# Chunk-selecting attention and a mixture of experts: rows of tokens placed into expert tables during the attention instead of gathered after it

## The chip, the cores and the metric

The kernel runs on one core of a Trainium2 chip. The metric is the device time of one execution in microseconds. Before the change it is 395.49 us (median of 3 runs, 395.29 to 395.6). A core has five engines that run side by side and meet at semaphores: TensorE (PE) multiplies matrices into PSUM; VectorE (DVE) and ScalarE (ACT) work on tiles in SBUF and PSUM; GpSimd (POOL) works on SBUF and issues DMAs, among them indirect ones, whose rows are picked by a list of indices; SyncE (SP) issues plain DMAs. Sixteen DMA engines move the data.

## The reference, cut to what matters

Attention: 4 batches, 8 heads, 768 positions, 64 channels. Keys lie in 24 chunks of 32. For each query an upper bound of its score against each chunk is computed from the chunk's smallest and largest keys, the 6 chunks with the largest bounds are kept, and a causal softmax attention runs over those alone.

```python
ub = np.sum(np.maximum(q[:, :, :, None, :] * k_min[:, :, None, :, :], q[:, :, :, None, :] * k_max[:, :, None, :, :]), axis=-1)
ub = np.where(causal, ub, -1000000000.0)
top_chunks = np.argsort(ub, axis=-1)[..., -top_k:]
scores = scale * np.matmul(q, k.transpose(0, 1, 3, 2))
mask = sel & (pos[:, None] >= pos[None, :])
# ... softmax over the masked scores, times v
```

Its outputs are 3072 tokens of 512 channels. Each goes through a dense two-layer network and through one of 8 expert networks of the same shape, the one with the largest logit:

```python
y_dense = np.maximum(x @ w1_dense, 0.0) @ w2_dense
expert_idx = np.argmax(x @ w_gate, axis=1)
# for each expert e, over the tokens that chose it (mask):
h = np.maximum(x[mask] @ w1[e], 0.0)
y_moe[mask] = gate_w[mask, None] * (h @ w2[e])
# ...
return y_dense + y_moe
```

The experts' tokens are worked on in blocks of 128 rows of one expert. With any split of 3072 tokens over 8 experts there are at most 24 + 7 = 31 blocks.

## The kernel before

It has three stages. First, attention, two heads ("a pair") at a time, 16 pairs, 11 "units" of scores each. While a batch's attention runs, the dense work of the batch before it is filled in. Then the last batch's dense work and the routing. Then 31 blocks of expert work.

Loading and casting of a pair, and what is prepared from it:

```python
def load(p):
    # ... for k, q, v and both heads:
    nc.sync.dma_start(out=f[:, g], in_=src[b, 2 * hp + g].rearrange("(t p) d -> p t d", p=128))

def cast(p):
    # ... three GpSimd copies from fp32 to fp16: k16, q16, v16

def prep_k(p):
    # ... six transposes of k16 into pk, in PSUM
    nc.vector.tensor_reduce(out=ks[:, 0, :], in_=pkc, op=ALU.max, axis=mybir.AxisListType.X)
    nc.vector.tensor_reduce(out=ks[:, 1, :], in_=pkc, op=ALU.min, axis=mybir.AxisListType.X)
    # ...
    nc.vector.tensor_copy(kT[p % NB][0][64:128, :], pk[0:64])
    nc.vector.tensor_copy(kT[p % NB][1][0:64, :], pk[64:128])

# prep_q: transposes of q, its positive part by ScalarE, its negative part by VectorE
# prep_ub: bounds by matmuls, VectorE's max of 8 for the sixth largest, flags of dropped chunks
# prep_s: twelve transposes (six for each head) and a 128x768 copy for each head
```

Scores, outputs and the end of a pair. The flags lie beside the queries in the moving matrix and rows of -30000 beside the keys, so that dropped chunks vanish in the exponential:

```python
def scores(p, u):
    # ... matmuls of up to 512 columns into sp
    nc.scalar.activation(ex[:, :o], sp[:, :o], AF.Exp, scale=0.125)
    # ... where a tile lies on the diagonal:
    nc.gpsimd.affine_select(out=exd, in_=exd, compare_op=ALU.is_ge, fill=0.0, base=0,
                            pattern=[[0, n], [1, 128]], channel_multiplier=-1)

def av(p, u):
    if u == 0:
        s["op"] = pout.tile([128, 2, 512], FP, name="op")   # pout has one buffer
    # ... matmuls of ex with v into op

def norm(p):
    nc.vector.reciprocal(rs, opv[:, :, :, D : D + 1])
    nc.vector.tensor_tensor(xbig[...], opv[:, :, :, 0:D], rs.to_broadcast([128, 2, NT, D]), ALU.mult)
```

A batch's tokens and dense outputs are stored to two DRAM tensors, `xd` (fp16 rows and the gate's weight) and `yd` (fp32). After attention the routing finds, from one-hot matrices of all 3072 tokens, the list of tokens of every block, and the blocks run:

```python
def gather(i):
    nc.gpsimd.indirect_dma_start(out=xg, in_=xd, in_offset=...gi[:, i : i + 1]...)
    nc.gpsimd.indirect_dma_start(out=yg, in_=yd, in_offset=...gi[:, i : i + 1]...)

# tx(i): four transposes of xg, copied to SBUF by VectorE
# e1(i): four matmuls with the expert's first weights, relu by ScalarE
# th(i): four transposes, copied by ScalarE

def e2(i):
    # ... four matmuls with the expert's second weights into yp
    nc.vector.scalar_tensor_tensor(o, yp, s["x"][:, Dm : Dm + 2].bitcast(FP), s["y"], ALU.mult, ALU.add)
    nc.gpsimd.indirect_dma_start(out=out, out_offset=...si[:, i : i + 1]..., in_=o, ...)

gather(0); gather(1); tx(0)
for i in range(NBLK):
    e1(i)
    # ... gather(i + 2), tx(i + 1), e2(i - 1)
    th(i)
```

The offset of a block's expert in the weights is in a register of PE, all 31 loaded at once before the blocks.

Of the kernel before, what the change touches and what calls it, by code (L numbers as in the profile page):

```python
# [17 lines left out]
def kernel(  # L18
# [31 lines left out]
    xd = dram.tile([N, XW], U16, name="xd")  # L50
    yd = dram.tile([N, Dm], FP, name="yd")
# [4 lines left out]

    exf = const.tile([32, S], HF)
    nc.gpsimd.memset(exf, -30000.0)
    nc.gpsimd.affine_select(out=exf, in_=exf, compare_op=ALU.is_ge, fill=0.0,
                            base=0, pattern=[[1, S]], channel_multiplier=-32)  # L60
    nc.gpsimd.affine_select(out=exf, in_=exf, compare_op=ALU.is_ge, fill=0.0,
                            base=31, pattern=[[-1, S]], channel_multiplier=32)

    cbias = const.tile([128, NT, 2, NC], HF)
    nc.gpsimd.memset(cbias, 0.0)
    for g in range(2):
        nc.gpsimd.affine_select(out=cbias[:, :, g, :], in_=cbias[:, :, g, :], compare_op=ALU.is_ge,
                                fill=-60000.0, base=0, pattern=[[128, NT], [-32, NC]], channel_multiplier=1)


    hmask = const.tile([128, 2, NC], HF)
    nc.gpsimd.memset(hmask, 0.0)
    nc.gpsimd.memset(hmask[0:64, 0, :], 1.0)
    nc.gpsimd.memset(hmask[64:128, 1, :], 1.0)

    NB = 3
    kT = [[const.tile([128, S], HF, name=f"kT{i}_{g}") for g in range(2)] for i in range(NB)]
    q16 = [const.tile([128, NT, 256], HF, name=f"q16_{i}") for i in range(NB)]
    v16 = [const.tile([128, 2, NT, D + 1], HF, name=f"v16_{i}") for i in range(NB)]
    for i in range(NB):  # L80
        nc.vector.memset(kT[i][0], 0.0)
        nc.vector.memset(kT[i][1], 0.0)
        nc.vector.tensor_copy(kT[i][0][0:32, :], exf)
        nc.vector.tensor_copy(kT[i][1][64:96, :], exf)
        nc.gpsimd.memset(q16[i], 0.0)
        nc.gpsimd.memset(v16[i][:, :, :, D : D + 1], 1.0)
# [3 lines left out]
    nc.gpsimd.iota(iom8, pattern=[[0, NT], [1, E]], base=-E, channel_multiplier=0, allow_small_or_imprecise_dtypes=True)  # L90
    ohp = const.tile([128, E, NM + 1], HF)
    nc.gpsimd.memset(ohp, 0.0)
    segm = const.tile([128, E, NM + 1], FP)
    nc.gpsimd.memset(segm, 1.0)
    nc.gpsimd.memset(segm[:, :, 0:1], 0.0)
    ones = const.tile([128, 128], HF)
    nc.gpsimd.memset(ones, 1.0)
    low = const.tile([128, 128], HF)
    nc.gpsimd.memset(low, 1.0)
    nc.gpsimd.affine_select(out=low, in_=low, compare_op=ALU.is_gt, fill=0.0,  # L100
                            base=0, pattern=[[1, 128]], channel_multiplier=-1)
    io128 = const.tile([128, 128], HF)
    nc.gpsimd.iota(io128, pattern=[[1, 128]], base=0, channel_multiplier=0, allow_small_or_imprecise_dtypes=True)
    ioblk = const.tile([128, NBLK], HF)
    nc.gpsimd.iota(ioblk, pattern=[[1, NBLK]], base=0, channel_multiplier=0, allow_small_or_imprecise_dtypes=True)
    iom1 = const.tile([128, NM], HF)
    nc.gpsimd.iota(iom1, pattern=[[1, NM]], base=1, channel_multiplier=0, allow_small_or_imprecise_dtypes=True)
    iop = const.tile([128, 1], FP)
    nc.gpsimd.iota(iop, pattern=[[0, 1]], base=0, channel_multiplier=1, allow_small_or_imprecise_dtypes=True)

    xbig = const.tile([128, NM, XW], HF)
    nc.gpsimd.memset(xbig[:, :, Dm:XW], 0.0)
# [6 lines left out]
    def load_dense():  # L119
        nc.gpsimd.dma_start(out=wg, in_=moe_w_gate.rearrange("(ko ki) e -> ki ko e", ki=128))  # L120
        nc.gpsimd.dma_start(out=wd[:, 0:NK], in_=moe_w1_dense.rearrange("(ko ki) f -> ki ko f", ki=128))
        nc.gpsimd.dma_start(out=wd[:, NK:], in_=moe_w2_dense.rearrange("(ko ki) f -> ki ko f", ki=128))

    def load_expert(e, w):
        src = moe_w1 if w == 0 else moe_w2
        nc.gpsimd.dma_start(out=we[:, e, w * NK : (w + 1) * NK], in_=src[e].rearrange("(ko ki) f -> ki ko f", ki=128))
# [3 lines left out]
    PIECES = [  # L130
        [(0, 0, 512)],
        [(1, 128, 640)],
        [(0, 512, 768), (4, 512, 768)],
        [(2, 256, 768)],
        [(1, 640, 768), (3, 384, 768)],
    ]
    units = []
    for pc in PIECES:
        for g in range(2):
            units.append([(g,) + x for x in pc])  # L140
    units.append([(g, 5, 640, 768) for g in range(2)])
    first_of = {}
    last_of = {}
    for u, un in enumerate(units):
        o = 0
        for g, bb, a, z in un:
            for t in range(a // 128, z // 128):
                last_of[g, t] = (u, bb)
    NU = len(units)

    mh = ctx.enter_context(tc.tile_pool(name="mh", bufs=2))
    my = ctx.enter_context(tc.tile_pool(name="my", bufs=3))
    mg = ctx.enter_context(tc.tile_pool(name="mg", bufs=2))
    mx = ctx.enter_context(tc.tile_pool(name="mx", bufs=2))

    fills = []
# [14 lines left out]

    def batch_fills(b):
# [4 lines left out]
        def xtr(mi):  # L177
            def f():
                tp = ptile("tr", [128, NK, 128], HF, "tp")
                for ko in range(NK):  # L180
                    nc.tensor.transpose(tp[:, ko], xbig[:, b * NT + mi, ko * 128 : (ko + 1) * 128], ident)
                nc.vector.tensor_copy(xT[:, :, mi * 128 : (mi + 1) * 128], tp)
            return f

        def gate():
            lg = ptile("tr", [128, NT, E], FP, "lg")
            for mi in range(NT):
                for ko in range(NK):
# [12 lines left out]
            nc.vector.tensor_tensor(ohp[:, :, 1 + b * NT : 1 + (b + 1) * NT].rearrange("p e t -> p t e"),  # L201
                                    iom8, mn.unsqueeze(2).to_broadcast([128, NT, E]), ALU.is_equal)
            ss = mg.tile([128, NT, 1], FP, name="ss")
            nc.vector.tensor_reduce(out=ss, in_=el, op=ALU.add, axis=mybir.AxisListType.X)
            nc.vector.reciprocal(xbig[:, b * NT : (b + 1) * NT, Dm : Dm + 2].bitcast(FP), ss)
            nc.sync.dma_start(out=xd[b * S : (b + 1) * S].rearrange("(m p) w -> p m w", p=128),
                              in_=xbig[:, b * NT : (b + 1) * NT].bitcast(U16))
# [14 lines left out]
        def l2(g, i, hold):  # L222
            def f():
# [7 lines left out]
                nc.sync.dma_start(out=yd[m * 128 : (m + 1) * 128], in_=ys)  # L231
# [12 lines left out]
        return out_list, dense  # L244

    with (
        tc.tile_pool(name="aload", bufs=3) as aload,
        tc.tile_pool(name="ahead", bufs=2) as ahead,
        tc.tile_pool(name="aexp", bufs=5) as aexp,
        tc.tile_pool(name="psc", bufs=3, space=bass.MemoryType.PSUM) as psc,  # L250
        tc.tile_pool(name="pout", bufs=1, space=bass.MemoryType.PSUM) as pout,
# [3 lines left out]
        st = [dict() for _ in range(NP)]  # L255

        def load(p):
            b, hp = divmod(p, HP)
            for nm, src in (("k", k), ("q", q), ("v", v)):
                f = aload.tile([128, 2, NT, D], FP, name=nm + "f")  # L260
                st[p][nm] = f
                for g in range(2):
                    nc.sync.dma_start(out=f[:, g], in_=src[b, 2 * hp + g].rearrange("(t p) d -> p t d", p=128))

        def cast(p):
# [3 lines left out]
            nc.gpsimd.tensor_copy(q16[p % NB][:, :, 64:192].rearrange("p t (g d) -> p t g d", g=2),  # L269
                                  s["q"].rearrange("p g t d -> p t g d"))  # L270
            nc.gpsimd.tensor_copy(v16[p % NB][:, :, :, 0:D], s["v"])

        def prep_k(p):
            s = st[p]
            pk = pprep.tile([128, S], HF, name="pp")
            for t in range(NT):
                nc.tensor.transpose(pk[:, t * 128 : (t + 1) * 128], s["k16"][:, t].rearrange("p g d -> p (g d)"), ident)
            ks = ahead.tile([128, 2, NC], HF, name="ks")
            pkc = pk.rearrange("d (c w) -> d c w", w=32)
            nc.vector.tensor_reduce(out=ks[:, 0, :], in_=pkc, op=ALU.max, axis=mybir.AxisListType.X)  # L280
            nc.vector.tensor_reduce(out=ks[:, 1, :], in_=pkc, op=ALU.min, axis=mybir.AxisListType.X)
            s["kb"] = kb = ahead.tile([128, 2, 2, NC], HF, name="kb")
            nc.vector.tensor_tensor(kb, ks.unsqueeze(2).to_broadcast([128, 2, 2, NC]),
                                    hmask.unsqueeze(1).to_broadcast([128, 2, 2, NC]), ALU.mult)
            nc.vector.tensor_copy(kT[p % NB][0][64:128, :], pk[0:64])
            nc.vector.tensor_copy(kT[p % NB][1][0:64, :], pk[64:128])

        def prep_q(p):
            s = st[p]
            pq = pprep.tile([128, S], HF, name="pp")  # L290
            for t in range(NT):
                nc.tensor.transpose(pq[:, t * 128 : (t + 1) * 128], q16[p % NB][:, t, 64:192], ident)  # L292
            s["qp"] = qp = ahead.tile([128, S], HF, name="qp")
            nc.scalar.activation(qp, pq, AF.Relu)  # L294
# [131 lines left out]
        while wq:  # L426
            load_expert(*wq.pop(0))
# [180 lines left out]
```

## Time and profile before

| | |
|---|---|
| time | 395.49 us, median of 3 runs |
| span of the profiled execution | 392.8 us |
| busy: PE, DVE, ACT, POOL | 258.8, 192.1, 159.7, 208.0 us |
| moved by DMA | 56.92 MB in 98370 packets, 78462 of them under 512 B |
| attention, first scores to last pair's end | 28.2 to 213.4 us |
| routing and the last batch's dense work | 213.4 to 238.6 us |
| blocks, first transposes to last result | 238.6 to 383.8 us |

The profile is one execution. Its rows of tenths cut the span into 40 slices of 9.8 us: a digit is an engine's busy share there. A group line has a source line, engine, operation, output and input with shapes and a count; then busy time and mean duration; then how long the engine was idle just before these instructions, and who ended that. A timeline line has start and duration in us first, and in brackets the idle time before it and who ended it. Shares over the whole span say little here: the stages have different limits.

### The profile page before, as it was taken

The page shows a single profiled execution, that of the slowest core. Times are in us where ns is not written, and L with a number is a line of the kernel's source. Part 1 is how long each engine was busy: PE and PEld are TensorE (multiplying, and loading weights), DVE is VectorE, ACT ScalarE, POOL GpSimd, SP SyncE. Part 2 cuts the span into 40 slices and gives each one's busy share as a digit, 9 for nine tenths or more (in the row PEclk, how much of TensorE's full clock was granted, in tenths as well). Part 3 has the DMA queues.
Part 4 walks back from the last instruction along what each step waited for, and adds up shares of the span by engine and source line. Part 5 has one row for each costly group of instructions (what it writes and reads, how often), then busy time and mean ns, then how long its engine had stood idle before and what let it go on. Part 6 is the DMA issues. An engine that isn't in the chain of part 4 may idle for free. (4 is left out here: it accounts for less than half of the span.)

```text
span 392.8 us, 7052 instructions
## 1 busy us (share of the span) xinstructions
PE 258.8 (66%) x2426; PEld 152.8 (39%) x2426; DVE 192.1 (49%) x538; ACT 159.7 (41%) x303; POOL 208.0 (53%) x370
## 2 busy tenths in 40 slices
PE   0157377157599989999898872667555658565660
PEld 0135254045365666666665531333222323222230
DVE  8284438248387798777952890222222323232220
ACT  1016257056276867787675320322132222322230
POOL 9946185174455555554322025366756656666541
PEclk9998869779699999999999996888989996989895
DMA  9999999999997886211031425143444444444440
GB/s 182 208 222 214 208 204 198 170 199 204 222 236 191 190 200 145 94 53 56 3 119 49 164 106 173 42 154 114 131 133 132 149 145 135 134 136 133 128 121 0
DMA packets 98370, 56.92 MB, mean 145 GB/s; under 512 B 78462, under 2 KB 90750, under 8 KB 98336
## 3 DMA queue, kind: packets, MB, share of 16 engines
q1 hardware_dynamic: 81856, 28.42, 32.8%
q0 software_dynamic: 16480, 28.06, 30.1%
q8 instruction: 20, 0.33, 0.3%
q14 instruction: 14, 0.11, 0.1%
HBM read 50.08 MB, written 17.66 MB: 172 GB/s over the span
## 5 line engine op out<-in xcount | busy, mean ns | idle before, releaser
L334 ACT ACTIVATE ex<-sp 128x512 f16<-128x512 f32 (+1 forms) x176 | 91.7, 585 | 63.1 <-PE sp L330 31.1
L344 POOL TENSOR_SCALAR_AFFINE_SELECT ex<-ex 128x128 f16<-128x128 f16 (+1 forms) x176 | 52.2, 306 | 55.9 <-ACT ex L334 53.0
L362 PE MATMUL op<-v,ex 128*128 128x65 f16 x672 | 47.6, 200 | 34.6 <-POOL ex L344 29.7
L330 PE MATMUL sp<-r,kT 128*128 128x512 f16 (+3 forms) x256 | 65.1, 328 | 3.6 <-ACT ex L334 2.1
L362 PEld LDWEIGHTS <-ex 128*128 128x128 f16 x672 | 37.3, 101 | 49.5 <-POOL ex L344 35.0
L535 DVE COPY exT<-tp 128x512 f16<-128x512 f16 x31 | 13.2, 425 | 80.5 <-PE tp L533 59.3
L523 POOL DMA_INDIRECT xg<-xd,gi x31 | 30.3, 977 | 41.5 <-DVE yo L561 21.6
L552 ACT COPY ehT<-tp 128x512 f16<-128x512 f16 x31 | 18.2, 586 | 74.2 <-PE tp L550 67.9
L541 PE MATMUL hp<-we,exT 128*128 x124 | 37.4, 432 | 10.2 <-DVE exT L535 5.8
L558 PE MATMUL yp<-we,ehT 128*128 x124 | 38.8, 419 | 4.5 <-ACT ehT L552 2.6
L533 PE MATMUL tp<-ident,xg 128*128 128x128 f16 x124 | 14.2, 247 | 40.7 <-DMA xg<-xd,gi 40.7
L562 POOL DMA_INDIRECT out_dram<-yo,si x31 | 31.5, 1015 | 15.3 <-issue 13.4
L561 DVE SCALAR_TENSOR_TENSOR yo<-yp,xg,yg 128x512 f32<-128x512 f32 x31 | 23.3, 750 | 31.9 <-PE yp L558 27.2
L526 POOL DMA_INDIRECT yg<-yd,gi x31 | 29.4, 949 | 10.5 <-issue 10.2
L322 DVE COPY r<-pp 128x768 f16<-128x768 f16 x32 | 17.0, 554 | 32.8 <-PE pp L320 32.6
L544 ACT ACTIVATE eh<-hp 128x512 f16<-128x512 f32 x31 | 18.5, 597 | 35.2 <-PE hp L541 26.3
L533 PEld LDWEIGHTS <-xg 128*128 128x128 f16 x124 | 8.3, 108 | 56.9 <-DMA xg<-xd,gi 56.8
L217 PE MATMUL hp<-xT,wd 128*128 128x384 f16 x128 | 26.5, 325 | 0.7 <-ACT hT L219 0.3
L330 PEld LDWEIGHTS <-kT 128*128 128x128 f16 x256 | 21.8, 103 | 11.1 <-issue 8.2
L226 PE MATMUL yp<-wd,hT 128*128 128x512 f16 x96 | 24.6, 378 | 1.5 <-DVE xbig L371 1.0
L269 POOL CAST q<-qf 128x768 f16<-128x768 f32 x16 | 13.3, 831 | 21.5 <-DMA qf<-in_q_dram 20.9
L294 ACT ACTIVATE qp<-pp 128x768 f16<-128x768 f16 x16 | 13.0, 810 | 23.1 <-PE pp L292 23.1
(115 smaller groups left out, 431.0 us busy)
## 6 DMA issues: line engine op xcount, KB each, us to landing
we<-in_moe_w_dram POOLq DMA_DIRECT2D x16, 512.0 KB
kf<-in_k_dram SPq DMA_DIRECT2D x32, 192.0 KB, 4.4
qf<-in_q_dram SPq DMA_DIRECT2D x32, 192.0 KB, 4.5
vf<-in_v_dram SPq DMA_DIRECT2D x32, 192.0 KB, 4.7
yd<-ys SPq DMA_DIRECT2D x24, 256.0 KB, 2.1
xd<-xbig SPq DMA_DIRECT2D x4, 792.0 KB, 4.3
wd<-in_moe_w_dense_dram POOLq DMA_DIRECT2D x2, 512.0 KB
xg<-xd,gi POOLq DMA_INDIRECT x31
```

Of the source, the lines that this page charges most:

```text
L217: nc.tensor.matmul(hp, wd[:, ko, j * 128 : (j + 1) * 128], xT[:, ko, g * G * 128 : (g + 1) * G * 128], start=(ko == 0), stop=(ko == NK - 1))
L226: nc.tensor.matmul(yp, hold["h"][:, j, i * 128 : (i + 1) * 128], wd[:, NK + j], start=(j == 0), stop=(j == NK - 1))
L330: nc.tensor.matmul(sp[:, o : o + z - a], kT[p % NB][g][:, bb * 128 : (bb + 1) * 128], s["r", g][:, a:z], start=(o == 0), stop=True, skip_g ...
L334: nc.scalar.activation(ex[:, :o], sp[:, :o], AF.Exp, scale=0.125)
L344: nc.gpsimd.affine_select(out=exd, in_=exd, compare_op=ALU.is_ge, fill=0.0, base=0, pattern=[[0, n], [1, 128]], channel_multiplier=-1)
L362: nc.tensor.matmul(op[:, g, t * (D + 1) : (t + 1) * (D + 1)], ex[:, c : c + 128], v16[p % NB][:, g, bb, :], start=(u == g and n == 0), sto ...
L523: nc.gpsimd.indirect_dma_start(out=xg, out_offset=None, in_=xd, in_offset=bass.IndirectOffsetOnAxis(ap=gi[:, i : i + 1], axis=0))
L526: nc.gpsimd.indirect_dma_start(out=yg, out_offset=None, in_=yd, in_offset=bass.IndirectOffsetOnAxis(ap=gi[:, i : i + 1], axis=0))
L541: nc.tensor.matmul(hp, s["xT"][:, ko], wef[:, bass.ds(offs[i] + ko * 512, 512)], start=(ko == 0), stop=(ko == NK - 1))
L558: nc.tensor.matmul(yp, s["hT"][:, j], wef[:, bass.ds(offs[i] + (NK + j) * 512, 512)], start=(j == 0), stop=(j == NK - 1))
L561: nc.vector.scalar_tensor_tensor(o, yp, s["x"][:, Dm : Dm + 2].bitcast(FP), s["y"], ALU.mult, ALU.add)
L562: nc.gpsimd.indirect_dma_start(out=out, out_offset=bass.IndirectOffsetOnAxis(ap=si[:, i : i + 1], axis=0), in_=o, in_offset=None, bounds_c ...
```

## The change

It rebuilds how tokens reach their experts, and a good part of the attention around it.

1. **A table in place of lists.** DRAM holds one table with room for every token under each expert. When a batch's gate is known, each of its tokens gets its row: its expert's base and its rank among the tokens so far. Six indirect DMAs, one for each tile of 128 tokens, write fp16 rows, gate weight and token number there; each is issued behind a causal mask of the scores, at intervals, during the next batch's attention. The last batch's are issued behind blocks' outputs.
2. **Blocks are plain reads.** 128 rows of the table are read by SyncE at an address in a register, up to eight blocks ahead. The first N1 = 11 blocks are full with tokens of the first three batches and start without the last batch. Blocks 29 to 31 run only where they are needed.
3. **Outputs are added.** The dense outputs are stored straight into the output; a block's result is scaled and added to it by an indirect DMA that accumulates. `yd`, its gathers and the two-operand end of a block go.
4. **The last batch** has its dense work, gate and placing spread over the first blocks.
5. **Attention.** Tokens are laid out so that a partition reads two neighbouring rows of k and q at once (512 B; v stays at 256 B). The transposed keys are copied to SBUF once by ScalarE and reduced there. The flags of both heads share one tile (six transposes for twelve). All four of the first diagonal tiles of a head lie in one unit, so that there are three masks of 512 columns for a pair in place of eleven smaller ones. Outputs lag one unit behind, into a PSUM tile for each head, two in all.
6. **Start.** The first two pairs' loads are issued before the constants; constants of the routing come in pair 2; weights are loaded from pair 1 (dense) and pairs 2 to 13 (experts), each tied to a cast.

The core of the diff, cut:

```diff
-    xd = dram.tile([N, XW], U16, name="xd")
-    yd = dram.tile([N, Dm], FP, name="yd")
+    CAP = N + 128
+    EMPTY = E * CAP
+    table = dram.tile([EMPTY + 128, XW], U16, name="table")
+    N1 = (N * (B - 1) // B - E * 127 + 127) // 128
+    N2 = NBLK - N1
...
+                    nc.sync.dma_start(out=f[:, g].rearrange("p (T j) d -> p T (j d)", j=NJ),
+                                      in_=src[b, 2 * hp + g].rearrange("(T p j) d -> p T (j d)", p=128, j=NJ))
...
+    def expand(i):
+        nc.scalar.copy(kT[i][0][64:96, :], exf[0:32])
+        nc.scalar.copy(kT[i][1][0:32, :], exf[0:32])
...
+        def ranks():
+            # one-hot rows times a triangle of ones, plus bases and counts so far: each token's row
...
+        def place(t):
+            def f():
+                with tc.issue_after(latest["pool"].ins):
+                    put(t)
+            return f
+        def put(t):
+            sc = nc.gpsimd.indirect_dma_start(
+                out=table, out_offset=bass.IndirectOffsetOnAxis(ap=keep["slot"][:, t : t + 1], axis=0),
+                in_=xbig[b % 2][:, t].bitcast(U16), in_offset=None)
...
-                nc.sync.dma_start(out=yd[m * 128 : (m + 1) * 128], in_=ys)
+                for j in range(NJ):
+                    st_ = nc.sync.dma_start(out=outv[m, j], in_=ys[64 * j : 64 * j + 64])
...
+        at.setdefault(9, []).append(ranks)
+        for t in range(NT):
+            at.setdefault(11 + 5 * t, []).append(place(t))
...
+    def fetch(i):
+        es[i]["x"] = xg = eg.tile([128, XW], U16, name="xg")
+        ld = nc.sync.dma_start(out=xg, in_=table[bass.ds(rows[i], 128)])
...
-        tc.tile_pool(name="pout", bufs=1, space=bass.MemoryType.PSUM) as pout,
+        tc.tile_pool(name="pout", bufs=2, space=bass.MemoryType.PSUM) as pout,
...
+            s["kp"] = kp = ahead.tile([128, S], HF, name="kp")
+            nc.scalar.copy(kp.rearrange("d (T p j) -> d T p j", p=128, j=NJ),
+                           pk.rearrange("d (T j p) -> d T p j", p=128, j=NJ))
...
-                nc.gpsimd.affine_select(out=exd, in_=exd, compare_op=ALU.is_ge, fill=0.0, base=0,
-                                        pattern=[[0, n], [1, 128]], channel_multiplier=-1)
+            if pc[0][1] == pc[0][2]:
+                latest["pool"] = nc.gpsimd.affine_select(out=ex, in_=ex, compare_op=ALU.is_ge, fill=0.0, base=0,
+                                        pattern=[[0, 4], [1, 2], [2, 64]], channel_multiplier=-1)
...
-            nc.vector.scalar_tensor_tensor(o, yp, s["x"][:, Dm : Dm + 2].bitcast(FP), s["y"], ALU.mult, ALU.add)
+            nc.vector.tensor_scalar(o, yp, s["x"][:, Dm : Dm + 2].bitcast(FP), None, ALU.mult)
+            sc = nc.gpsimd.indirect_dma_start(
+                out=out, ..., in_=o, ..., compute_op=ALU.add)
...
+        extra = {0: a[:NT] + [a[NT], ranks], 1: places[:2], 2: places[2:4], 3: places[4:] + [empty]}
+        for n, f in enumerate(d):
+            extra.setdefault(1 + n * (N1 - 2) // len(d), []).append(f)
```

## The prediction, made before the changed kernel ran

> **What bounds the kernel now.** I read the slices of the span first, since shares over the whole span mix three stages.
>
> ```profile
> PE   0157377157599989999898872667555658565660
> POOL 9946185174455555554322025366756656666541
> PEclk9998869779699999999999996888989996989895
> DMA  9999999999997886211031425143444444444440
> ```
>
> One digit is 9.8 us. Three stages stand out. Up to about 120 us the DMA row is full while PE has holes; from 120 to 210 us PE is nearly full and DMA is free; from 240 us on no engine is full.
>
> Next the start, on the timeline of 0 to 32 us.
>
> ```profile
> 12.73 0.41 POOL L112 MEMSET xbig<- 128x384 f16 x1
> ...
> 15.56 0.87 POOL L268 CAST k<-kf 128x768 f16<-128x768 f32 x1
> ...
> 28.18 0.58 PE L330 MATMUL sp<-r,kT 128*128 128x512 f16 x1
> ```
>
> GpSimd writes constants and issues weight loads until 15.56 us without a gap, so the first cast waits for GpSimd and not for data. First scores: 28.2 us.
>
> Then the VectorE timeline, the one line that ends each of the 16 head pairs.
>
> ```profile
> 60.82 0.96 DVE L371 TENSOR_TENSOR xbig<-op,rs 128x768 f16<-128x768 f32 x1
> 69.29 0.96 DVE L371 TENSOR_TENSOR xbig<-op,rs 128x768 f16<-128x768 f32 x1
> ...
> 89.19 0.96 DVE L371 TENSOR_TENSOR xbig<-op,rs 128x768 f16<-128x768 f32 x1
> ...
> 105.78 0.95 DVE L371 TENSOR_TENSOR xbig<-op,rs 128x768 f16<-128x768 f32 x1
> ...
> 115.27 0.96 DVE L371 TENSOR_TENSOR xbig<-op,rs 128x768 f16<-128x768 f32 x1
> ```
>
> Between 115.27 and 196.09 us eight pairs take 10.1 us each. Early ones take 15.7, 19.9 and 16.6 us (pair 2 alone took 8.5): 22 us of waits for loads. The last ends at 213.4 us.
>
> The table by stage says what fills the 10.1 us, and that the blocks are filled by nothing (columns: stretch, length, busy PE, PEld, DVE, ACT, POOL; clock; DMA share; GB/s):
>
> ```profile
> 150.00:190.00 40.00, 36.66 (x458) 24.18 (x456) 32.71 (x102) 29.27 (x59) 20.27 (x53) 1.00 0.22 72
> 300.00:340.00 40.00, 25.08 (x142) 11.43 (x142) 9.67 (x17) 10.56 (x18) 26.18 (x27) 0.91 0.45 144
> ```
>
> Last, GpSimd's timeline in the block stage and two groups of the page:
>
> ```profile
> 301.06 0.98 POOL L523 DMA_INDIRECT xg<-xd,gi  x1 [0.31 <-DVE exT L535]
> ...
> 302.35 0.95 POOL L526 DMA_INDIRECT yg<-yd,gi  x1 [0.30 <-issue]
> ...
> 303.60 1.02 POOL L562 DMA_INDIRECT out_dram<-yo,si  x1 [0.30 <-issue]
> ...
> 306.51 0.98 POOL L523 DMA_INDIRECT xg<-xd,gi  x1 [1.89 <-DVE yo L561]
> ```
>
> ```profile
> L533 PE MATMUL tp<-ident,xg 128*128 128x128 f16 x124 | 14.2, 247 | 40.7 <-DMA xg<-xd,gi 40.7
> L562 POOL DMA_INDIRECT out_dram<-yo,si x31 | 31.5, 1015 | 15.3 <-issue 13.4
> ```
>
> Three indirect DMAs per block, 1.28 us apart, are 3.85 us; then GpSimd waits for a block's result before it may gather again, and PE waits 40.7 us in all for gathered rows. A block takes 4.6 us ((374.1 - 251.0) / 27 between gathers). Between attention's end and the first block's transposes (213.4 to 238.6 us) lie routing and the last batch's dense layers.
>
> **What the Trainium skill says.** (1) "DMA: Bandwidth & Descriptors", Specifications: full rate needs transfers of 512 B or more. This trace agrees in direction: k, q and v arrive in 256 B packets of 21 ns (60 to 120 us, 203 GB/s), while packets of 1056 B take 48 to 52 ns. (2) Same page, "SWDGE vs HWDGE vs iDMA": a DMA that accumulates must be issued from GpSimd. The new kernel's does; the page gives no rate, and no run shows one yet. (3) "TensorE: Matmul & The Clock Gate", "What's actually happening": the PE clock halves after idle windows. The trace has a granted clock of 1.00 in 150 to 190 us and 0.91 in the blocks, where PE waits. (4) "ScalarE: Activation LUTs", "What ACT_TABLE_LOAD costs": neighbouring ACTIVATEs overlap by about 93 ns. The trace agrees: an exp of 512 columns takes 605 ns, five in a row 2.55 us, 0.51 each.
>
> **The change, part by part.**
>
> Start. Constants for routing move behind pair 2's start, weight loads too, and most memsets go to VectorE. GpSimd has left: identity (to 2.0 us in this trace), one causal mask in two halves (2 x 0.89), two selects of 0.81, so it is free near 5.5 us; two casts (0.87 each) end near 7.5. But ScalarE now first does six 32x768 copies of the mask rows (about 0.8 each, my estimate from its 128x768 at 0.81), to 10.4 us, and the key copy (0.81) waits behind them. Then as before: two chunk reductions 1.9, bounds with nine more matmuls 1.5, ten maxima 1.0, flags 0.4, transposes and three copies 2. First scores near 17 us instead of 28.2.
>
> Loads. k and q come in 512 B packets, for which I estimate 30 ns from the two sizes above: 24,576 x 30 / 16 engines = 46 us of packet time, v 24,576 x 21 / 16 = 33, weights (1,024 B packets, 98 ns) 57: 136 against 156 now. The 156 took about 137 us. Weights are now tied to pairs 1 to 13, not taken as early as GpSimd can, so the same queue is 80% used over the stage instead of full at its start. I take the 22 us of waits as gone.
>
> Attention, work per pair. ScalarE: the same 5,376 columns of exp, 0.51 x 10.5 = 5.4, the positive queries 0.72, new the key copy 0.72, and 1.2 of dense layers: 8.0 us. VectorE: two key reductions, now from SBUF, 1.85; bounds' masks 0.5; kT 0.7; r0 0.55; maxima 0.9; flags 0.4; three r copies 1.45; norm in two halves 1.4; sum 7.75 against 7.7 now. PE by its cadence (four matmuls of 512 columns take 1.02 us and one 0.38, so 0.213 each; eleven transposes 0.78 and one 0.22, so 0.056; 20 output matmuls 0.77, some 0.035): 5,376 score columns 2.24, 42 output matmuls 1.5, 18 transposes 1.0 (24 now), bounds 0.7, a quarter of a batch's dense work (12.8: 32 matmuls of 384 columns 5.1, 24 of 512 5.1, transposes, gate and ranks 2.6) 3.2: 8.6 as now. GpSimd: three selects of 512 columns, about 0.64 each (from 128 columns 295 ns and 256 columns 409 ns), in place of 3.4 us; casts 2.5; 1.5 placements of 1.3 us. So no engine's work falls much; what falls is the wait at pair boundaries: outputs get a PSUM tile per head, two in all, in place of one of both heads, and outputs lag a unit behind the scores. I put a pair with dense work at 9.6 us and the first four, without, at 8.3; the last two have no preparation (3 us less): 4 x 8.3 + 12 x 9.6 - 3 = 145 us, against 185 now.
>
> Routing. Rows go to a table of experts by rank, batch by batch, so the chain of 24 mask-and-matmul steps, the gathers and the third stage's index arithmetic go. The first N1 = (2304 - 1016 + 127) // 128 = 11 blocks need no row of the last batch. 25 us between attention and blocks become about 2; but 13 us of PE work of it (dense 10.2, transposes 1.35, gate and ranks 1.3) move among the first blocks.
>
> Blocks. With these inputs the experts' counts fill 28 blocks, so the last 3 of 31 are skipped. Per block PE needs 8 matmuls of 512 columns at 0.213 and 8 transposes at 0.056: 2.15 us; ScalarE 1.2, VectorE 1.1, GpSimd 1.3 (one indirect DMA). Rows come by SP, up to eight blocks ahead. I allow 2.5 us for a block. Offsets are loaded into PE's registers four at a time: one load of 31 took 2.80 us here, so I estimate 0.7 each, seven of them, 5 us. 28 x 2.5 + 13 + 5 = 88, against 144 now (238.6 to 383.0).
>
> End: 10 us now, 10 after. Sum: 17 + 145 + 2 + 88 + 10 = 262 us of span; the median lies 2.7 above this trace's span: **265 us**.
>
> **Rivals.**
>
> A. The adding write is the block stage's bound. A plain pair of 2 KB rows takes 164 ns now, 64 of them per block: 64 x 164 / 16 = 0.66 us. Reading the target first may double it, which hides beside 2.15 us of PE. At four times it is 2.6 us plus 0.4 of fetches, 3.0 a block, some 10 us more: 275. At eight times 5.6 a block: 28 x 5.6 = 157, some 335. Nothing in this profile shows such a DMA.
>
> B. Attention does not get below 10.1 us with dense work, because ScalarE's extra copy makes three engines equally full, or because the indirect placements hold up the masks on GpSimd: 12 x 0.5 plus 4 x 1.5, 277 us. For it: PE 92%, VectorE 82%, ScalarE 73% busy in 150 to 190 us.
>
> C. DMA remains the early bound, the placements and dense outputs adding to it: 15 us of the 22 stay, 280.
>
> D. Better than summed: the lag removes all boundary waits (9.0 a pair) and blocks run at 2.25: 265 - 7 - 7 = 251; with a start at 14, 248.
>
> **Range and chances.** A's mild form, B and C are each about one in four, and D as well; two of the first three together give about 290. Range 243 to 292. For no gain over 2%, well over 120 of the expected 130 us would have to vanish; only A's extreme form comes near. Faster 0.95, same 0.02, slower 0.03.
>
> **What would show it.** First scores near 17 us and casts before 9; VectorE's lines of pair ends 8 to 10 us apart from the first pair on, without one above 12; the DMA row in eights, not nines; one GpSimd DMA per block, blocks 2.3 to 2.7 us apart, granted clock 1.00 there; PE's wait for gathered rows under 5 us in all. I am wrong if PE waits in the blocks for fetches or free result buffers (then A), if pair ends stay 10 us or more apart (B), or if the casts wait for kf and qf (C).

## The result and the profile after

| | before | after |
|---|---|---|
| time, median | 395.55 us | 275.92 us (275.16 to 276.97) |
| ratio | | 0.697, interval 0.693 to 0.701 |
| span of the profiled execution | 392.8 us | 273.5 us |
| first scores | 28.2 us | 19.5 us |
| attention, to the end of PE's last output matmul | 184.0 us (28.2 to 212.2) | 159.7 us (19.5 to 179.2) |
| from there to the first block's transposes | 26.4 us | 2.5 us |
| blocks, from there to the start of the last result | 144.4 us (238.6 to 383.0) | 83.9 us (181.65 to 265.55) |
| moved by DMA | 56.92 MB | 49.64 MB |
| packets, of them under 512 B | 98370, 78462 | 75108, 29632 |

The slices of the span after; a digit is now 6.8 us:

```profile
PE   1159777888898968899995899939968999999970
DVE  6288999999989759998797997216634345545540
POOL 7565976546567656576827534400783445776662
PEclk9999999999999999999999999998999999999996
DMA  6999999998979989879996924256396999886875
```

PE is no longer at 5 and 6 in the last third: the blocks are filled by it. The holes in the first third are mostly gone, and the clock row is nines but for one 8 and the last slice. VectorE's row, not PE's, is the fullest in the first half of attention. The DMA row is still at nines there.

The start, on the timeline of all engines:

```profile
4.67 0.82 POOL L477 CAST k<-kf 128x768 f16<-128x768 f32 x1 [0.94 <-DMA kf<-in_k_dram]
...
10.57 0.83 ACT L146 COPY kT<-exf 32x768 f16<-32x768 f16 x1
11.30 0.78 ACT L492 COPY kp<-pp 128x768 f16<-128x768 f16 x1
...
12.12 1.81 DVE L496 TENSOR_REDUCE ks<-kp 128x24 f16<-128x768 f16 x2 [5.57 <-ACT kp L492]
...
19.48 1.44 PE L554 MATMUL sp<-rT,kT 128*128 128x128 f16 x6
```

The first cast runs at 4.7 us instead of 15.6 and now waits for data. ScalarE is in the way instead: its sixth mask-row copy (0.83 us each) ends at 11.4 us, and VectorE stands 5.6 us until the key copy behind them is done.

Pair ends on VectorE: the norm is now in two halves, and this is the second half of six of the pairs.

```profile
31.09 0.56 DVE L584 TENSOR_TENSOR xbig<-op,rs 128x384 f16<-128x384 f32 x1
...
41.84 0.56 DVE L584 TENSOR_TENSOR xbig<-op,rs 128x384 f16<-128x384 f32 x1
...
50.13 0.56 DVE L584 TENSOR_TENSOR xbig<-op,rs 128x384 f16<-128x384 f32 x1
...
58.42 0.56 DVE L584 TENSOR_TENSOR xbig<-op,rs 128x384 f16<-128x384 f32 x1
...
98.08 0.55 DVE L584 TENSOR_TENSOR xbig<-op,rs 128x384 f16<-128x384 f32 x1
...
113.36 0.56 DVE L584 TENSOR_TENSOR xbig<-op,rs 128x384 f16<-128x384 f32 x1
```

The second pair ends 10.7 us after the first, the third and fourth 8.3 us later each. The distance from 98.08 to 113.36, 15.3 us, belongs to a pair that starts a batch; the last pair that starts a batch takes 15.0.

The table by stage, with the columns of before (stretch, length, busy PE, PEld, DVE, ACT, POOL; clock; DMA share; GB/s):

```profile
20.00:55.00 35.00, 28.33 (x429) 20.91 (x428) 33.04 (x102) 29.88 (x57) 24.30 (x34) 1.00 1.10 219
55.00:95.00 40.00, 35.78 (x510) 25.58 (x510) 36.00 (x121) 30.89 (x62) 25.38 (x33) 1.00 0.98 213
225.00:262.00 37.00, 36.67 (x266) 20.48 (x265) 19.71 (x34) 19.58 (x34) 25.97 (x17) 1.00 0.83 139
```

VectorE is busy 33.04 of 35 us (94%) in the first pairs, and 36.00 of 40 in the next stretch. In the blocks PE is busy 99% at a clock of 1.00; before it was 25.08 of 40 us at 0.91. A DMA share over 1.00 means that summed packet times overlap.

GpSimd in the blocks, and PE's wait for rows, from the list of waits (total, times, longest):

```profile
258.01 1.55 POOL L715 DMA_INDIRECT out_dram<-yo,xg  x1 [0.62 <-DVE yo L714]
260.18 1.55 POOL L715 DMA_INDIRECT out_dram<-yo,xg  x1 [0.62 <-DVE yo L714]
```

```profile
PE tp L686 <- DMA xg<-table: 2.5, 1, 2.5
```

One indirect DMA a block instead of three, 2.17 us apart. It waits 0.62 us for the result, so GpSimd isn't what the blocks wait for in this stretch. PE's transposes wait for rows once, before the first block; before, 26 such waits cost 40.7 us. (A second bracket, 1.8 us, names a row read at the first expert matmul.)

### The profile page after: what moved, and what is told of

The parts are those of the page before. It is cut to its first block, busy times and chain, and to the rows that moved or that the text cites. A ratio compares the mean times of both kernels' runs of the same rounds, so it can differ in the third digit from the quotient of the medians.

```text
span 273.5 us, 7279 instructions
## 1 busy us (share of the span) xinstructions
PE 219.3 (80%) x2547; PEld 144.5 (53%) x2547; DVE 189.2 (69%) x587; ACT 170.8 (62%) x319; POOL 159.2 (58%) x197
## 2 busy tenths in 40 slices
DMA packets 75108, 49.64 MB, mean 182 GB/s; under 512 B 29632, under 2 KB 68160, under 8 KB 75072
## 5 line engine op out<-in xcount | busy, mean ns | idle before, releaser
L558 ACT ACTIVATE ex<-sp 128x512 f16<-128x512 f32 (+1 forms) x176 | 91.0, 595 | 17.7 <-PE sp L554 11.7
L554 PE MATMUL sp<-rT,kT 128*128 128x128 f16 (+3 forms) x384 | 63.5, 261 | 5.9 <-ACT ex L558 4.1
L715 POOL DMA_INDIRECT out_dram<-yo,xg x28 | 43.7, 1561 | 24.9 <-DVE yo L714 17.0
L560 POOL TENSOR_SCALAR_AFFINE_SELECT ex<-ex 128x512 f16<-128x512 f16 x48 | 32.3, 678 | 31.3 <-ACT ex L558 28.9
L378 POOL DMA_INDIRECT table<-xbig,slot x24 | 24.0, 999 | 26.3 <-DVE nf L334 15.4
L496 DVE TENSOR_REDUCE ks<-kp 128x24 f16<-128x768 f16 x32 | 29.2, 944 | 11.1 <-ACT kp L492 11.0
L714 DVE TENSOR_SCALAR yo<-yp,xg 128x512 f32<-128x512 f32 x28 | 21.0, 750 | 18.2 <-PE yp L711 12.2
L395 ACT ACTIVATE hT<-hp 128x384 f16<-128x384 f32 x32 | 15.8, 494 | 12.0 <-PE hp L393 10.8
L492 ACT COPY kp<-pp 128x768 f16<-128x768 f16 x16 | 12.9, 804 | 10.7 <-PE pp L490 10.7
L477 POOL CAST k<-kf 128x768 f16<-128x768 f32 x16 | 13.2, 826 | 9.8 <-PE pp L490 7.8
L584 DVE TENSOR_TENSOR xbig<-op,rs 128x384 f16<-128x384 f32 x32 | 17.6, 551 | 0.5
```

What stands on the lines that cost most here:

```text
L378: sc = nc.gpsimd.indirect_dma_start(out=table, out_offset=bass.IndirectOffsetOnAxis(ap=keep["slot"][:, t : t + 1], axis=0), in_=xbig[b % 2 ...
L496: nc.vector.tensor_reduce(out=ks[:, i], in_=kp.rearrange("d (c w) -> d c w", w=32), op=op, axis=mybir.AxisListType.X)
L554: nc.tensor.matmul(sp[:, o : o + w], kT[p % NB][g][:, kt * 128 : (kt + 1) * 128], rT[p % NB][g][:, a * 128 : z * 128], start=(o == 0), sto ...
L558: nc.scalar.activation(ex[:, 0:o], sp[:, 0:o], AF.Exp, scale=0.125)
L560: latest["pool"] = nc.gpsimd.affine_select(out=ex, in_=ex, compare_op=ALU.is_ge, fill=0.0, base=0, pattern=[[0, 4], [1, 2], [2, 64]], chan ...
L714: nc.vector.tensor_scalar(o, yp, s["x"][:, Dm : Dm + 2].bitcast(FP), None, ALU.mult)
```

## The experiments

All times are medians. A ratio is to the kernel before, run beside it; that kernel took 392.27 us beside experiments 4, 9, 11 and 12, and 395 to 397 us beside the others and the changed kernel. So a difference of medians between those four and the others can be off by some 3 us. Where that matters, the difference is given "by the ratios" too, that is, the difference of the two ratios times 395.55 us. "Undo" kernels start from the changed kernel, "alone" kernels from the one before.

### 1. The weights' timing alone

```diff
-                if wq:
-                    load_expert(*wq.pop(0))
                 if n2 is not None:
                     cast(n2)
+                    # dense weights behind pair 1's cast, experts' behind the casts of pairs 2 to 13
+                    with tc.issue_after(st[n2]["cast"].ins): ...
```

> The kernel before, with only its weight loads held back: dense weights behind pair 1's casts, one expert load a pair from pair 2, two from pair 10, each behind a cast, as in the changed kernel; k and q still come in 256 B packets. Theory (the early waits of 22 us came from weights taken too early): pair ends 10 to 11 us apart from the first on, 395.5 falls to 372 to 380 us. Rival (the small packets themselves cause them): the waits only move to later pairs, and the time stays above 388 us.

Measured: 366.63 us, ratio 0.926 (0.919 to 0.932). Nothing else of the change is in it. The table of the kernel before in 20 to 60 us, and its two longest waits for loads; then this kernel's table of 20 to 55 us:

```profile
20.00:60.00 40.00, 23.82 (x231) 16.75 (x231) 21.14 (x64) 16.06 (x30) 22.34 (x46) 0.83 1.21 212
...
POOL q L269 <- DMA qf<-in_q_dram: 20.9, 4, 7.6
...
POOL k L268 <- DMA kf<-in_k_dram: 8.1, 2, 5.3
```

```profile
20.00:55.00 35.00, 26.78 (x324) 17.60 (x322) 28.06 (x84) 22.30 (x42) 23.43 (x55) 1.00 1.26 212
```

The DMA share is as high and the 212 GB/s are the same: the queues move as much, but in another order. GpSimd's casts wait 0.9 us in all for k now, and not for q. PE is busy 26.78 of 35 us, and 23.82 of 40 before. The first six pair ends lie 8.6 to 9.7 us apart, later ones 7.6 to 12.3, and the last pair ends at 183.8 us instead of 213.4, 30 us earlier. That is more than was expected: the weights that were fetched early had taken the place of inputs that were needed first. Some 2.5 of the 30 us are the start (first scores at 25.7 us), where the dense weights' loads no longer stand ahead of the first cast on GpSimd.

### 2 to 4. The blocks, layer by layer

Plain reads in place of the gathers. This kernel, and the two that follow from it, read fixed rows and not the tokens of a block; only their times are read.

```diff
-            nc.gpsimd.indirect_dma_start(out=xg, out_offset=None, in_=xd, in_offset=...gi[:, i : i + 1]...)
+            r0 = (i % NM) * 128
+            nc.sync.dma_start(out=xg, in_=xd[r0 : r0 + 128])
```

> The kernel before, with both gathers of a block read by SyncE as 128 neighbouring rows (the rows are fixed, so the routing of tokens to blocks is left out of what is read); the bytes and the indirect store stay. Theory (a block costs what GpSimd's three indirect DMAs and their waits cost): with one left, blocks fall from 4.6 to 2.2 to 2.6 us, 31 x 2.2 = 68 us less: 323 to 335 us. Rival (the bytes moved, or PE's chain of four steps, bound a block): blocks stay above 3.5 us, time above 360 us.

Measured: 381.78 us, 0.955 (0.946 to 0.963). Two of its four executions, the profiled one among them, were slow, and the ratio is of the fast ones, which took 377.1 and 380.7 us. The theory falls: 18 us by the ratio (14 by the medians) instead of 60 to 70. The list of waits names the next bound.

```profile
POOL out_dram L561 <- DMA out_dram<-yo,si: 67.7, 21, 4.3
```

Stores wait for the one before to land, 67.7 us in 21 waits. They are 4.18 us apart on average, and were 4.43: the gathers had hidden this. The rival had the time right, not its reason.

Then the same with the stores freed of that order, which changes nothing in what is stored, since each token is in one block:

```diff
+            if i > 0:
+                tc.declare_no_dep(sc.ins, group="add", reason="every token is in one block")
+            tc.add_to_no_dep_group("add", sc.ins)
```

> The kernel before with plain reads in place of gathers (as in the run above), and its indirect stores free of order among themselves. Theory (gathers and the order of stores were two bounds, one under the other): blocks at 2.3 to 2.8 us, 318 to 338 us. Rival (three buffers of rows, or the bytes, bound a block): above 355 us.

Measured: 366.58 us, 0.930 (0.923 to 0.936). By the ratios that is 10 us below the kernel with ordered stores. It misses the 318 to 338 us too. Waits of this kernel:

```profile
PE tp L532 <- DMA xg<-xd: 28.7, 25, 2.2
```

Blocks are 3.70 us apart on average, in turns of about 2.1 and 5.5: rows may be fetched only when one of three row buffers is free, and PE waits for them 25 times, up to 2.2 us each. So the depth was tried, with more buffers and earlier reads together:

```diff
+        tc.tile_pool(name="egr", bufs=10) as egr,
-        gather(0)
-        gather(1)
+        for i in range(8):
+            gather(i)
-            if i + 2 < NBLK:
-                gather(i + 2)
+            if i + 8 < NBLK:
+                gather(i + 8)
```

> The kernel before with plain reads of fixed rows, stores free of order, and now ten buffers of rows, read eight blocks ahead, in place of three and two. Theory (a third bound lay under the two: three buffers, freed only by a block's end, so that a read's round trip of 2.5 to 4.5 us shows; without it PE is left): blocks from 3.7 to 2.2 to 2.5 us, 31 x 1.3 = 40 us less than the 366.6 us of the run with three buffers: 320 to 335 us. Rival (the bytes bound it: 0.6 MB a block): above 350 us.

Measured: 319.54 us, 0.815 (0.809 to 0.821), 47 us below the kernel without the depth by the medians and 45 by the ratios, where 40 were expected. The end of its block stage (columns as above):

```profile
300.00:312.00 12.00, 9.99 (x69) 5.24 (x67) 5.78 (x9) 5.31 (x9) 5.06 (x7) 1.00 0.24 86
```

The clock is 1.00. PE is busy all 50 us from 250 to 300, and 9.99 of the last 12, in which its work runs out. Four limits lay on top of one another: gathers (4.4 to 4.6 us a block), the order of stores (4.2), the row buffers (3.7), PE's own work (blocks are 2.17 us apart here). Taking one away gave 18, then 10, then 45 us, by the ratios.

### 5. Undo: the adding stores in order

```diff
-            apart(sc, "add", "every token is in one block")
```

> The changed kernel, with the blocks' adding stores put in order: each waits for the one before it to land, as the stores of the kernel before do. Theory (with the gathers gone the next bound under them is the order of the stores, which the changed kernel gives up as every token lies in one block): blocks fall back from 2.2 to 4 us or more, 28 x 1.8 = 50 us less the 13 us of stalls that the first blocks have anyway: 310 to 330 us. Rival (the order costs nothing, as it lies beside PE's work): under 4 us more.

Measured: 353.88 us, 0.894 (0.889 to 0.899), 78 us more than the changed kernel. GpSimd's timeline:

```profile
278.50 1.55 POOL L715 DMA_INDIRECT out_dram<-yo,xg  x1 [2.78 <-DMA out_dram<-yo,xg]
283.45 1.55 POOL L715 DMA_INDIRECT out_dram<-yo,xg  x1 [3.40 <-DMA out_dram<-yo,xg]
```

The bracket names the store before as the releaser. The results of the last 17 blocks are 5.42 us apart instead of 2.21, beyond the expectation: ordered stores that add lie further apart than the plain ones of experiment 2 (4.18). The clock falls with it, to 0.82 in 270 to 290 us. "TensorE: Matmul & The Clock Gate", section "What's actually happening", in the Trainium skill has the clock halve after idle stretches; this trace agrees in direction, with that number beside 1.00 in the changed kernel.

### 6. Stores that do not add

The dense outputs are left out of the rows that a block writes; the store replaces instead of adding.

```diff
-                bounds_check=N - 1, oob_is_err=False, compute_op=ALU.add)
+                bounds_check=N - 1, oob_is_err=False)
```

> The changed kernel, with blocks' results stored without the addition (the dense outputs are left out of these rows). Theory (blocks are bound by PE at 2.15 us; the longer issue on GpSimd, 1.55 us, lies beside it): 273 to 276 us. Rival (the adding DMA bounds the blocks): 5 us less or more, under 271.

Measured: 272.94 us, 0.693 (0.688 to 0.698), 3.0 us less. One issue costs 983 ns and not 1553. In the view of one line's instructions (shortest/median/longest ns, and when), the changed kernel, then this one:

```profile
L715 POOL DMA_INDIRECT out_dram<-yo,xg x28: 1553/1553/1610, 194.8 to 266.6; - x28
```

```profile
L715 POOL DMA_INDIRECT out_dram<-yo,xg x28: 983/983/1003, 194.2 to 265.1; - x28
```

The last blocks remain 2.19 us apart, so the issue is hidden. Rival A is out: adding costs some 3 us (1.7 by the ratios), and the two intervals overlap. The traces have the size that A asked for, too: a row of 2 KB that is added takes 178 ns of a DMA engine (median), a plain one of the dense outputs 84 ns, and a pair of plain rows in this kernel 169. That is the doubling of A's mild form, and it is hidden as A said.

### 7 and 8. VectorE as attention's bound

The two key copies of a pair made twice on VectorE (the second into a tile that nothing reads):

```diff
             nc.vector.tensor_copy(kT[p % NB][1][64:128], kp[64:128])
+            xk = ahead.tile([128, S], HF, name="xk")
+            nc.vector.tensor_copy(xk[0:64], kp[0:64])
+            nc.vector.tensor_copy(xk[64:128], kp[64:128])
```

> The changed kernel, with VectorE's two copies of the transposed keys (0.34 and 0.38 us) made a second time for each pair, into a tile nobody reads. Theory (in the changed kernel's attention VectorE is the bound, 90 to 94% busy): 16 x 0.72 = 11.5 us more, at least 8: 284 to 288 us. Rival (PE, ScalarE or the loads bound it and VectorE has room): under 3 us more, below 279 us.

Measured: 289.03 us, 0.729 (0.725 to 0.734), 13.1 us more; attention runs from 20.4 to 190.5 us. Two copies alone are 0.34 and 0.36 us, so 16 pairs added 11.2 us of work, and attention ends 11.3 us later: all of it came out. Work added to VectorE is on the path. That less work there would make attention shorter is not shown by it.

So the same two copies were taken off VectorE:

```diff
-            nc.vector.tensor_copy(kT[p % NB][0][0:64], kp[0:64])
-            nc.vector.tensor_copy(kT[p % NB][1][64:128], kp[64:128])
+            nc.gpsimd.tensor_copy(kT[p % NB][0][0:64], kp[0:64])
+            nc.gpsimd.tensor_copy(kT[p % NB][1][64:128], kp[64:128])
```

> The changed kernel, with the two key copies moved from VectorE to GpSimd. Theory (VectorE bound): some 0.7 us a pair less, 16 x 0.7 = 11 at most; GpSimd gets 2 x 0.5 us a pair and has room (64% busy), so 266 to 272 us. Rival (GpSimd's masks get late behind the copies, or VectorE is not the bound): 275 us or more.

Measured: 302.3 us, 0.760 (0.755 to 0.766), 26 us more. The theory falls, and whether attention gains from a lighter VectorE stays open, since this move loaded GpSimd instead. Its waits:

```profile
PE op L573 <- POOL ex L560: 28.0, 10, 7.0
...
POOL kT L506 <- DMA table<-xbig,slot: 18.9, 5, 7.4
```

A copy takes 0.82 us on GpSimd, so 16 pairs need 26 us there. Worse, GpSimd does its work in order: it stood 18.9 us at a key copy, and masks behind it came late, so PE waited 28.0 us for masked scores (5.3 in the changed kernel). "GPSIMD Engine Reference", section 4.1, in the skill calls operations of one input roughly line-rate; the measured 0.82 us beside 0.34 to 0.38 on VectorE decides here.

### 9. Packets of 256 B for k and q

```diff
-                    nc.sync.dma_start(out=... "p T (j d)" ...)
+                    for j in range(NJ):
+                        nc.sync.dma_start(out=... [:, :, j], in_=... [:, :, j])
```

> The changed kernel, with k and q read as twice as many transfers of 256 B packets into the same places. Theory (tied weights ended the early waits; packet size gives margin only): 276 to 281 us, as 20 us more packet time fit into a stage whose DMA row has room after 120 us. Rival (the packets of 512 B are what ended the waits): casts wait for kf and qf again, 286 us or more.

Measured: 287.57 us, 0.733 (0.728 to 0.739), 11.7 us more by the medians and 14.4 by the ratios: the rival's number. The casts wait for loads again:

```profile
POOL q L480 <- DMA qf<-in_q_dram: 13.8, 5, 6.7
POOL k L478 <- DMA kf<-in_k_dram: 9.2, 4, 3.8
```

Attention ends at 193.5 us instead of 179.2, 14.3 later. So size and timing both count, and neither makes the other idle. The kernel also issues twice as many loads; what part that has is not separated here.

### 10 and 11. The placements' spreading, and the copy of token numbers

All six placements of a batch at one step:

```diff
-            at.setdefault(11 + 5 * t, []).append(place(t))
+            at.setdefault(11, []).append(place(t))
```

> The changed kernel, with all six placements of a batch at one step of the attention (the eleventh) in place of one every five steps. Theory (what is spread are pauses of 1.3 us on GpSimd, behind which masks wait): six in a row hold the masks up to 7 us, of which two units ahead cover 2: 3 to 5 us in each of three batches, 9 to 15 more: 285 to 291 us. Rival (they fit anywhere, as GpSimd is 64% busy): 274 to 278 us.

Measured: 278.49 us, 0.705 (0.699 to 0.710), 2.6 us more, with intervals that overlap. The theory falls. GpSimd's timeline has the cost that was expected:

```profile
113.47 1.04 POOL L378 DMA_INDIRECT table<-xbig,slot  x1 [2.10 <-DVE rs L582]
...
119.92 0.96 POOL L378 DMA_INDIRECT table<-xbig,slot  x1 [0.30 <-DMA table<-xbig,slot]
...
123.07 0.74 POOL L560 TENSOR_SCALAR_AFFINE_SELECT ex<-ex 128x512 f16<-128x512 f16 x1 [0.37 <-ACT ex L558]
```

From the first placement to the next mask 9.6 us pass, and attention ends at 185.9 us, 6.7 later. But the pairs that start batches take 13.0 and 12.9 us instead of 15.3 and 15.0, and PE's first expert matmul follows attention by 2.35 us instead of 4.7. So something other than placements made those pairs long. GpSimd's timeline of the changed kernel, at the first of them:

```profile
98.82 0.26 POOL L292 COPY xbig<-num 128x6 int32<-128x6 int32 x1 [4.27 <-DMA table<-xbig,slot]
99.03 0.66 POOL L560 TENSOR_SCALAR_AFFINE_SELECT ex<-ex 128x512 f16<-128x512 f16 x1
```

A copy of 128x6 token numbers stands at the head of the queue for 4.27 us and holds the mask behind it; in the other long pair it is 4.77 us. It stands in the code at the end of the batch's gate, and its place in the queue is far ahead of the gate. What it waits for is less clear than the bracket: that names a placement's DMA here and a dense output's store in the other pair, but VectorE's last norm, which writes the same tile, ends at 98.63 us, just before the copy starts. Its place in the queue can be tested without settling that. It was tied behind a mask of its own gate's time:

```diff
-            nc.gpsimd.tensor_copy(xbig[b % 2][:, :, Dm + 2 : Dm + 4]..., num[:, b * NT : (b + 1) * NT])
+            with tc.issue_after(latest["pool"].ins):
+                nc.gpsimd.tensor_copy(xbig[b % 2][:, :, Dm + 2 : Dm + 4]..., num[:, b * NT : (b + 1) * NT])
```

> The changed kernel, with the copy of the token numbers into a batch's rows tied behind a mask of that batch's gate, where it had been issued early and stood 4.3 and 4.8 us on GpSimd waiting for the placements before it, masks behind it. Theory (GpSimd's punctuality for masks is what batch starts lose time on): 4 to 8 us less, 268 to 272 us. Rival (VectorE's gate chain is what fills those pairs of 15 us): no change, 274 to 277 us.

Measured: 267.6 us, 0.682 (0.679 to 0.686), 8.3 us less than the changed kernel by the medians and 5.8 by the ratios. GpSimd's timeline has the copy without a wait:

```profile
99.69 0.18 POOL L293 COPY xbig<-num 128x6 int32<-128x6 int32 x1
```

The long pairs take 13.0 and 12.9 us, as with the placements bunched, and attention ends at 175.0 us, 4.2 earlier. Those 4.2 us are the copy's. Another 2.7 us of the difference lie in the blocks, 79.0 us from the first expert matmul instead of 81.7. But experiment 9, whose kernel before also took 392.27 us, has 77.9 us there without this edit, while the changed kernel and experiments 6, 7, 8 and 10 have 79.9 to 82.8. So this part is not shown to be the copy's.

### 12. The best version

The copy tied; mask rows of only the first pair ahead of the first key copy; placements every four steps.

```diff
-        for i in range(NB):
-            expand(i)
+        expand(0)
         cast_qk(0)
...
         prep_ub(0)
+        expand(1)
+        expand(2)
...
-            at.setdefault(11 + 5 * t, []).append(place(t))
+            at.setdefault(11 + 4 * t, []).append(place(t))
```

> The changed kernel, with that copy tied; the last two of three copies of the mask rows behind the first pair's preparation; and placements every four steps in place of five. Theory: first scores at 16 us in place of 19.5, though VectorE has to make up its preparations, so only 1 to 3 us of it stay; the first block's rows are read some 4 us earlier, as they wait for the last placement, 2 to 4 us; with the copy 4 to 8: 262 to 268 us. Rival (VectorE fills attention whatever its start): 270 us or more.

Measured: 263.43 us, 0.671 (0.667 to 0.675), faster than both kernels: than the changed one by 12.5 us in the medians and 10.4 by the ratios. Its slices, at 6.6 us a digit:

```profile
PE   1366888778899999899999799979999989999960
DVE  6673989999998889998979999346753245555540
```

First scores are at 15.5 us instead of 19.5, the first expert matmul follows attention after 2.1 us instead of 4.7, and the last result is begun at 255.6 us. But attention still ends at 175.9 us, as with the copy alone (175.0): the 4 us of the start are given back in it. VectorE's row is at nines there; that it is what takes them back is argued from experiment 7, not isolated.

## Why the prediction was right, and where its sum was off

Predicted were 265.0 us in a range of 243 to 292; 275.92 came. The sum differs from the measured stages by few terms:

| term | predicted | measured |
|---|---|---|
| first scores | 17 | 19.5 |
| attention | 145 | 159.7 |
| to the first block, and blocks | 2 + 88 | 2.5 + 83.9 |
| end | 10 | 8.0 |
| span | 262 | 273.5 |

**Start: right, 2.5 us late.** The key copy does wait behind ScalarE's six copies, as written. They began at 6.30 us and ended 1 us later than estimated; the rest lies after the key copy.

**Loads: right in effect, wrong in a sign.** The 22 us of waits are gone, and the two reasons given are both shown: weights tied alone bring 30 us of attention's end, packets of 256 B alone cost 14.3. The estimate of 30 ns for a packet of 512 B held: the mean is 30.8. The DMA row was to be in eights; it is mostly in nines until about 150 us. With the row in nines, GpSimd's casts waited 3.1 us in all for k and q, so a full row alone did not show a bound.

**Attention: the mis-sized term, 14.7 us.** "So no engine's work falls much" and 8.3 us for a pair without dense work held for the third and fourth pair only. Two things were not in the sum. First, the pairs before them took 12.2 and 10.7 us, 6.3 us more: VectorE had still to prepare the following pairs while it served these (five preparations start on it in the time of the first four pairs, from 20.3 to 52.9 us). Its work per pair came to 8.3 to 8.5 us, where 7.75 were summed; doubling 0.7 us of it moved attention's end by 11.3. Second, the twelve pairs with dense work took (179.2 - 59.0) / 12 = 10.0 us and not 112 / 12 = 9.35, 8 us in all. Two of them lie above 12 us, which the text had said none would: 15.3 and 15.0, of which experiment 11 shows 2.3 and 2.1, over half of the 8, to come from the number copy at the head of GpSimd's queue. The rest fits VectorE's larger sum, and is not isolated; PE is as full in these pairs. Rival B comes nearest to all this: its 277 us is 1 us from the result, and its sign, pair ends 10 us or more apart, is half met, as the twelve pairs average 10.0, with seven of them shorter. It had put this down to three engines equally full or to placements that hold up masks. VectorE and PE are equally full in 55 to 95 us (36.00 and 35.78 of 40), but ScalarE, whose extra copy B named, is at 30.89. GpSimd's order was the right place to look, but the instruction was another, and bunching the placements costs only 2.6 us net. That B's number fits so well is in part luck.

**Routing and blocks: right.** The mechanism held in each part: one indirect DMA, rows ahead of need, clock 1.00, PE's wait for rows 2.5 us (4.3 with the second bracket) against "under 5". Blocks at 2.21 us (the last 17) lie under the 2.5 allowed, and near PE's sum of 2.15; the first ten, with the dense work among them, are 3.5 us apart. A register load of up to four took 0.51 us in the mean and not 0.7. Nearly right is the way to the first block, 2.5 us and not 2, which is PE's wait for the first rows. With the placements over earlier, in experiments 10 and 12, the block follows sooner. Whether their landing or SyncE's own load of the rows' addresses, from 177.4 to 179.3 us just ahead of the read, held that read is not separated. The 24 us won between attention and blocks, and the 8.7 us at the start, are read from the two traces; no experiment takes either away alone.

**Adding: right, with one wrong size that did not count.** An issue of 1.55 us stands where 1.0 was assumed. It lies beside 2.2 us of PE and is hidden (experiment 6). Had the stores been kept in order, though, the changed kernel would stand at 353.88 us; the prediction never named this term. It was right because the kernel declares its stores independent.

## What to carry to other kernels

When a wait is taken away, ask what lies directly under it: here the limits of gathers, store order and row buffers lay within 1 us a block of one another, so the first two steps gave 18 and 10 us, and the third 45. Before a queue is called the bound because it is full, look at its order: the same bytes with the weights held back ended attention 30 us earlier. And on an engine that works in order and has a part in the critical chain, look at what stands at the head of its queue: a copy of 0.26 us, issued too early, stood there for 4.27 and 4.77 us with masks behind it, and cost attention 4.2 us.

## What the runs showed of the hardware

- An indirect DMA of 128 rows keeps GpSimd 0.98 us, or 1.55 us when it accumulates; 0.30 us lie between two in a row.
- Indirect stores of 128 rows of 2 KB, each waiting for the one before to land, came 4.18 us apart when plain (some of them waited for other things) and 5.42 us apart when adding.
- An added row of 2 KB took 178 ns of a DMA engine, a plain one 84 ns; a packet of 256 B took 21 to 22 ns in the mean, one of 512 B 30.8.
- A copy of 64x768 in fp16 takes 0.82 us on GpSimd, and on VectorE 0.34 to 0.38.
- A load of three or four registers took 0.33 to 0.78 us on PE; one of 31 took 2.80.
